# Twelve gated tiles of a fused attention and mixture kernel: split into two f16 words and turned by DMA instead of by TensorE

## The chip, the core and the metric

One Trainium2 chip, of which the kernel uses one core. The metric is the device time of one launch in microseconds (us), taken from the first to the last work of the core. The kernel before was run three times.

## What is computed

The reference is three layers, one after the other; `x` is 2304 tokens (4 batches of 576) by 512.

```python
# layer 0: attention with decay, 4 batches x 8 heads, 576 rows, 64 wide
scores = (q @ k.T) / 8 + cum[:, None] - cum[None, :]      # cum = cumsum(log f); causal mask
x = softmax(scores) @ v                                   # -> [2304, 512]
# layer 1: one dense gated block
h = x @ w_in                                              # w_in [512, 2048]
g = h * sigmoid(1.702 * h)
x = g @ w_out                                             # w_out [2048, 512]
# layer 2: soft mixture of 8 experts, 4 slots each
logits = x @ phi                                          # phi [512, 32]
slots = softmax(logits, over tokens).T @ x                # 32 slots
slot_out[e] = relu(slots[e] @ w1[e]) @ w2[e]
out = softmax(logits, over slots) @ slot_out
```

Layer 1's output is never formed. The kernel folds `w_out @ phi` into one matrix `wphi` [2048, 32], so that the logits of a token are its row of `g` times `wphi`, and it sums the rows of `g` itself for the slots; `w_out` is applied to 32 slot sums at the end.

## The kernel before, in words

The tokens are 18 blocks of 128, and two blocks make a chunk: 9 chunks, 0 to 8. Layer 1 works on a chunk in eight **units** `(t, fg)`: block `t` of the chunk (0 or 1) and a quarter `fg` of the 2048 columns. I number the units through: chunk 2 is units 16 to 23, chunk 4 is 32 to 39, chunk 6 is 48 to 55, the last one is 71. A unit (`moe_steps`, L797) is:

- twelve f16 products `hp` of 128x512 on PE (L814 to L816), three for each of four slices of the inner dimension, since tokens and weights are each held in a high and a low f16 word;
- the gate: `tanh` on ACT (L829), then a product on DVE (L830), which leaves the tile `g`, 128 tokens by 512 in f32;
- later, the **turn** (`turn`, L758): four f32 transposes of 128x128 on PE into one PSUM bank `gT` (L766), and a copy on ACT into `gt` (L773; three buffers);
- later still, the **product with wphi** (`by_phi`, L779): four f32 matmuls whose 32 output columns go to four different groups of 32 PSUM partitions of the tile `p4` (the traces call it `p`, L788). The four groups are added up afterwards (`slot_steps`, L880) by a matmul with `rsum`.

A unit is turned when a later one has been issued, and its product waits for the turn after that (`held`). When all units of a chunk are through, `slot_steps` takes the logits, the softmax over tokens and the slot sums `sp` (L954).

Attention runs interleaved with layer 1: `attend` hands out pieces between the half units, by a table of costs. From the sixth row block on (`late`), a piece (`emit_qk`, L540) is scores on PE, their maximum on DVE (L577), `exp` on ACT (L581), a split of the probabilities into two f16 words `pn` (ACT L589 for the high word, DVE L590 for the low one; two buffers), a DMA transpose into `ph` (L594; three buffers), and the products with `vv` on PE (L632 to L634). The turned queries and keys `kab`, `qa`, `qb` come by DMA transposes too (L347).

All loads and all DMA transposes are issued by SP's queue, in order. The order on each engine is not the order of the code: a scheduler that keeps a timeline of its own sets it when the kernel is built. Each engine then works through its list without overtaking.

The pool `ap_` holds what attention needs, and the buffers `low` of the weight preparation. When the last piece of attention is issued it is closed, and the memory goes to tiles `we` for the expert weights (33 MB in 128 loads, L1109 to L1114), so the first of them waits until attention's tiles are free.

Of the kernel before, what the change touches and what calls it, by code (L numbers as in the profile page):

```python
# [10 lines left out]
F32 = mybir.dt.float32  # L11
# [9 lines left out]
WS = 256.0  # L21
# [9 lines left out]
def attention_moe_softmoe(ctx, tc, q, k, v, f, w_in, w_out, phi, w1, w2, out):  # L31
# [131 lines left out]
    w_at, w_loaded = [0], [0]  # L163
    W_AHEAD = 7

    N_LOW = 2
    RAW_AT = (7, 6, 5, 4, 3, None, None, 7, 6, None, None, 7, None, None, None, None)
    wo_pair = {}

# [28 lines left out]
    def w_first(n):  # L198


        if n in W32:
            nc.scalar.activation(out=W32[n], in_=W32[n], func=AF.Copy, scale=WS)
            return
        words = w_raw.pop(n).rearrange("p (n w) -> p n w", w=2)
        lo, hi = words[:, :, 0], words[:, :, 1]
        val = W32[n] = w32_tile(n)
        low = ap_.tile([128, 512], U32, tag="low", name="low", bufs=N_LOW)
        if n % 2 < 1:
            nc.gpsimd.tensor_scalar(out=val, in0=hi.bitcast(F32), scalar1=2.0 ** -111, scalar2=None, op0=ALU.mult)
        else:  # L210
            nc.scalar.activation(out=val, in_=hi.bitcast(F32), func=AF.Copy, scale=2.0 ** -111)
        nc.scalar.activation(out=low, in_=lo, func=AF.Copy, scale=0.93 * 2.0 ** -29)
        bits = val.bitcast(U32)
        nc.vector.scalar_tensor_tensor(
            out=low, in0=bits, scalar=3, in1=low, op0=ALU.logical_shift_left, op1=ALU.bitwise_or
        )
        nc.vector.scalar_tensor_tensor(
            out=bits, in0=bits, scalar=0x80000000, in1=low, op0=ALU.bitwise_and, op1=ALU.bitwise_or
        )
# [519 lines left out]

    G = {}
    P4 = {}
    held = deque()
# [6 lines left out]
    def units(c):  # L751
# [3 lines left out]
            return [(t, 2 * b + a) for b in range(2) for t in range(2) for a in range(2)]  # L755
        return [(t, fg) for t in range(2) for fg in range(FG)]

    def turn(c, t, fg):  # L758


        g = G[c, t, fg]
        pt = pt2 = ps_mm("gT")
        if (c, t, fg) == (NCH - 1, 1, FG - 1):
            pt2 = ps_sc("gT")
        for a in range(4):
            last_turn[0] = nc.tensor.transpose((pt if a < 2 else pt2)[:, a * 128:(a + 1) * 128], g[:, a * 128:(a + 1) * 128], ident)  # L766
        gt = mp.tile([128, 512], F32, tag="gt", name="gt", bufs=N_GT)
        if (c, t, fg) == (NCH - 1, 1, FG - 1):
            nc.scalar.copy(out=gt[:, halves[0]], in_=pt[:, halves[0]])
            nc.vector.tensor_copy(gt[:, halves[1]], pt2[:, halves[1]])  # L770
            warm(2)
        else:
            nc.scalar.copy(out=gt, in_=pt)  # L773
        with tc.issue_after(last_turn[0].ins):
            while held:
                by_phi(*held.popleft())
        held.append((c, t, fg, gt))
        if c == NCH - 1:
            by_phi(*held.popleft())  # L779

    def by_phi(c, t, fg, gt):
        one = c == NCH - 1
        first = units(c)[0] if not one else (t, 0)
        if (t, fg) == first:
            P4[c, t if one else 0] = (ps_sc if one and t else ps_mi)("p4")
        p4 = P4[c, t if one else 0][:, 0 if one else 128 * t:][:, 0:128]
        for a in range(4):
            last_p4[0] = nc.tensor.matmul(  # L788
                p4[NS * a:NS * (a + 1)], lhsT=wphi[:, 4 * fg + a, :], rhs=gt[:, a * 128:(a + 1) * 128],
                start=((t, fg) == first), stop=(fg == FG - 1), skip_group_check=True,  # L790
            )
        turned[c, t] = turned.get((c, t), 0) + 1
        ts = (t,) if one else (0, 1)
        if all(turned.get((c, i), 0) == FG for i in ts):
            for _ in slot[0]:
                pass
            slot[0] = slot_steps(c, ts)  # L797
            next(slot[0])

    def moe_steps(c):  # L800
        xt = XT[c]
        for u, (t, fg) in enumerate(units(c)):
            if c < 2:
                more_w((max(6, 4 * u + 4) if u < 4 else 16 + 2 * (u - 3)) if c == 0 else 24 + 2 * u + 2)
            hp = ps_mm("hp")
            ts = slice(t * 128, (t + 1) * 128)
            final = (c, u) == (NCH - 1, N_UNIT - 1)
            for kk in range(KD):
                if final and kk == KD - 1:
                    behind = last_turn[0]  # L810
                elif kk % 2 == 0:
                    behind = last_xT.pop(0) if last_xT else None
                with tc.issue_after(behind.ins) if behind else nullcontext():
                    nc.tensor.matmul(hp, lhsT=xt[:, 0, kk, ts], rhs=win(0, fg, kk), start=(kk == 0), stop=False)  # L814
                    nc.tensor.matmul(hp, lhsT=xt[:, 0, kk, ts], rhs=win(1, fg, kk), start=False, stop=False)  # L815
                    last_hp[0] = nc.tensor.matmul(  # L816
                        hp, lhsT=xt[:, 1, kk, ts], rhs=win(0, fg, kk), start=False, stop=(kk == KD - 1)
                    )
                if kk == 1:
                    if final:  # L820
                        while turns:
                            turn(*turns.popleft())
                    yield
            if fg % 2 == 0:
                for half in "ab" if (c, u) == (NCH - 1, 0) else "ab"[fg // 2]:
                    if (c, t, half) not in G:
                        G[c, t, half] = mp.tile([128, 2, 512], F32, tag="g", name="g", bufs=N_G)
            g = G[c, t, fg] = G[c, t, "ab"[fg // 2]][:, fg % 2]
            nc.scalar.activation(out=g, in_=hp, func=AF.Tanh, scale=0.851 / (VS * WS))  # L829
            nc.vector.scalar_tensor_tensor(out=g, in0=g, scalar=1.0, in1=hp, op0=ALU.add, op1=ALU.mult)  # L830
            turns.append((c, t, fg))
            for _ in range(min(3 if c < 2 else 2, len(turns) - 1)):
                if turns[0][2] >= folded[0]:
                    break
                turn(*turns.popleft())
            if c == NCH - 1:
                load_to(RING_AT[u])
            yield
# [4 lines left out]
    def warm(k):  # L843

        if not k:
            return
        if not idle:
            idle.append(ps_pv("z").rearrange("p (k n) -> p k n", k=4))
        for _ in range(k):
            tc.keep_in_program_order(  # L850
                nc.tensor.matmul(
                    idle[0], lhsT=ident16, rhs=ident16.unsqueeze(1).to_broadcast([128, 4, 128]), start=True, stop=True
                )
            )
# [23 lines left out]
    def slot_steps(c, ts=(0, 1)):  # L878
# [3 lines left out]
        end = c == NCH - 1 and ts[-1] == 1  # L882
        l4 = mp.tile([128, 256], F32, tag="l4", name="l4", bufs=1)[:, 0:128 * nt]
        nc.vector.tensor_scalar(
            out=l4, in0=P4.pop((c, ts[0]))[:, 0:128 * nt], scalar1=1.0 / (GS * WS), scalar2=None, op0=ALU.mult
        )
        lg = ps_mi("lg")
        lT = lg[:, 0:128 * nt]
# [477 lines left out]
```

## Time and profile before

| | us |
|---|---|
| median of three runs (lowest, highest) | 548.83 (547.62, 551.03) |
| the profiled execution | 544.7 |
| its span, first to last instruction | 542.2 |

The profiled execution is 4.1 us faster than the median, and what lies around its span is 2.5 us. Busy times are unions of instruction records; matmuls are pipelined, so that records of PE overlap, and what one costs in a full pipe is the distance from its start to the next start, not its length.

### The profile page before, as it was taken

The page shows a single profiled execution, that of the slowest core. Times are in us where ns is not written, and L with a number is a line of the kernel's source. Part 1 is how long each engine was busy: PE and PEld are TensorE (multiplying, and loading weights), DVE is VectorE, ACT ScalarE, POOL GpSimd, SP SyncE. Part 2 cuts the span into 40 slices and gives each one's busy share as a digit, 9 for nine tenths or more (in the row PEclk, how much of TensorE's full clock was granted, in tenths as well). Part 3 has the DMA queues.
Part 4 walks back from the last instruction along what each step waited for, and adds up shares of the span by engine and source line. Part 5 has one row for each costly group of instructions (what it writes and reads, how often), then busy time and mean ns, then how long its engine had stood idle before and what let it go on. Part 6 is the DMA issues. An engine that isn't in the chain of part 4 may idle for free.

```text
span 542.2 us, 13552 instructions
## 1 busy us (share of the span) xinstructions
PE 492.7 (91%) x5353; PEld 309.1 (57%) x5353; DVE 350.4 (65%) x898; ACT 310.6 (57%) x607; POOL 71.5 (13%) x123
## 2 busy tenths in 40 slices
PE   3467899999889999999999999989999999999982
PEld 3456776866567555655665657556665555454531
DVE  8988979778666447667677868877675413360132
ACT  5867686778667446556666667576664323221211
POOL 4866754311000000010000001000000000000000
PEclk9969799999999999999999999999999999999997
DMA  9998763999959307997739699994554499989998
GB/s 242 285 376 149 200 129 133 272 191 204 169 105 168 61 19 139 185 181 139 125 77 181 116 189 176 212 156 88 93 105 90 132 383 367 348 308 367 337 327 269
DMA packets 230847, 105.62 MB, mean 195 GB/s; under 512 B 202593, under 2 KB 213345, under 8 KB 230785
## 3 DMA queue, kind: packets, MB, share of 16 engines
q1 hardware_dynamic: 229552, 103.59, 80.3%
q10 hardware_dynamic: 1232, 1.18, 0.7%
q8 instruction: 42, 0.69, 0.6%
q14 instruction: 21, 0.16, 0.1%
HBM read 64.63 MB, written 4.72 MB: 128 GB/s over the span
## 4 chain that ended last, share of the span: by engine, by line
PE 65%; DMA 15%; DVE 9%; ACT 4%; SPq 2%; issue 2%; POOL 0%; DVEq 0%; ACTq 0%; POOLq 0%
PE hp L814 10%; PE hp L815 9%; PE hp L816 9%; DMA ph<-pn 6%; PE gT L766 5%; PE p L788 4%; DMA we<-in_moe_w_dram 3%; PE pv L626 3%; PE l L1227 3%; PE sp L954 3%; PE pv L632 2%; DMA kf<-in_k_dram 2%; PE scs L554 2%; DMA kab<-kan 2%; PE scs L555 2%
## 5 line engine op out<-in xcount | busy, mean ns | idle before, releaser
L814 PE MATMUL hp<-w,xt 128*128 128x512 f16 x288 | 109.6, 381 | 0.6 <-DVE g L830 0.6
L815 PE MATMUL hp<-w,xt 128*128 128x512 f16 x288 | 109.2, 379 | 0.0
L816 PE MATMUL hp<-w,xt 128*128 128x512 f16 x288 | 109.2, 379 | 0.0
L581 ACT ACTIVATE pf<-scs,mx 128x512 f32<-128x512 f32 (+3 forms) x108 | 57.3, 541 | 38.7 <-DVE mx L577 29.4
L830 DVE SCALAR_TENSOR_TENSOR g<-g,hp 128x512 f32<-128x512 f32 x72 | 49.2, 683 | 43.9 <-ACT g L829 43.7
L590 DVE SCALAR_TENSOR_TENSOR pn<-pf,pn 128x512 f16<-128x512 f32 (+2 forms) x78 | 51.2, 658 | 32.1 <-ACT pn L589 31.4
L829 ACT ACTIVATE g<-hp 128x512 f32<-128x512 f32 x72 | 42.5, 590 | 47.4 <-PE hp L816 47.3
L589 ACT ACTIVATE pn<-pf 128x512 f16<-128x512 f32 (+2 forms) x78 | 47.3, 607 | 22.3 <-DMA ph<-pn 19.8
L577 DVE CUSTOM_DVE_ANT_0 scs<-scs,zmq 128x128 f32<-128x128 f32 (+3 forms) x96 | 46.6, 496 | 6.8 <-PE scs L555 4.2
L773 ACT COPY gt<-gT 128x512 f32<-128x512 f32 x71 | 41.1, 582 | 10.7 <-PE gT L766 10.5
L816 PEld LDWEIGHTS <-xt 128*128 128x128 f16 x288 | 28.2, 98 | 32.9
L632 PE MATMUL pv<-vv,ph 128*128 128x65 f16 (+1 forms) x360 | 41.8, 196 | 5.3 <-DMA ph<-pn 4.2
L814 PEld LDWEIGHTS <-xt 128*128 128x128 f16 x288 | 28.8, 100 | 28.8 <-issue 5.0
L766 PE MATMUL gT<-ident,g 128*128 128x128 f32 x288 | 45.0, 277 | 0.0
L766 PEld LDWEIGHTS gT<-ident,g 128*128 128x128 f32 x288 | 34.0, 141 | 14.8 <-issue 3.5
L632 PEld LDWEIGHTS <-ph 128*128 128x128 f16 (+1 forms) x360 | 33.8, 102 | 14.6 <-issue 7.0
L815 PEld LDWEIGHTS <-xt 128*128 128x128 f16 x288 | 28.2, 98 | 23.7 <-issue 1.1
L633 PE MATMUL pv<-vv,ph 128*128 128x65 f16 (+1 forms) x360 | 41.7, 195 | 0.0
L634 PE MATMUL pv<-vv,ph 128*128 128x65 f16 (+1 forms) x360 | 41.4, 194 | 0.0
L588 POOL MEMSET pn<- 128x128 f16 x12 | 2.5, 205 | 252.6 <-DMA ph<-pn 250.8
L633 PEld LDWEIGHTS <-ph 128*128 128x128 f16 (+1 forms) x360 | 34.1, 102 | 2.5 <-issue 0.6
L554 PE MATMUL scs<-kab,qa 128*128 128x128 f16 x240 | 34.4, 220 | 0.5 <-ACT pf L581 0.5
(233 smaller groups left out, 1017.3 us busy)
## 6 DMA issues: line engine op xcount, KB each, us to landing
we<-in_moe_w_dram SPq DMA_DIRECT2D x127, 256.0 KB, 5.5
raw<-in_moe_w_in_dram SPq DMA_DIRECT2D x16, 512.0 KB, 7.2
raw<-in_moe_w_out_dram SPq DMA_DIRECT2D x16, 512.0 KB, 5.7
kf<-in_k_dram SPq DMA_DIRECT2D x13, 256.0 KB, 3.3
qf<-in_q_dram SPq DMA_DIRECT2D x13, 256.0 KB, 3.7
vf<-in_v_dram SPq DMA_DIRECT2D x12, 256.0 KB, 4.2
out_dram<-ob SPq DMA_DIRECT2D x12, 256.0 KB, 3.5
ph<-pn SPq DMA_TRANSPOSE x78, 3.0
```

Source lines behind the costliest of these rows:

```text
L554: nc.tensor.matmul(o, lhsT=QA[r][:, h, :], rhs=KA[base + j][:, h, :], start=True, stop=False)
L577: nc.vector.tensor_tensor_reduce(out=o, in0=o, in1=mask, scale=-SC, scalar=3.0e38 if n == 128 else DG[r][1][:, u], op0=ALU.add, op1=ALU.mi ...
L581: nc.scalar.activation(out=pf[:, hh * nb:(hh + 1) * nb], in_=o, func=AF.Exp, bias=mx[:, hh:hh + 1], scale=-1.0)
L589: nc.scalar.activation(out=pn[:, 0, 0:w], in_=pf, func=AF.Copy, scale=PB)
L590: nc.vector.scalar_tensor_tensor(out=pn[:, 1, 0:w], in0=pf, scalar=PB, in1=pn[:, 0, 0:w], op0=ALU.mult, op1=ALU.subtract)
L632: nc.tensor.matmul(o, lhsT=ph[0:rr, 0, off:off + n], rhs=vh, start=(j == 0), stop=False)
L633: nc.tensor.matmul(o, lhsT=ph[0:rr, 0, off:off + n], rhs=vl, start=False, stop=False)
L766: last_turn[0] = nc.tensor.transpose((pt if a < 2 else pt2)[:, a * 128:(a + 1) * 128], g[:, a * 128:(a + 1) * 128], ident)
L814: nc.tensor.matmul(hp, lhsT=xt[:, 0, kk, ts], rhs=win(0, fg, kk), start=(kk == 0), stop=False)
L815: nc.tensor.matmul(hp, lhsT=xt[:, 0, kk, ts], rhs=win(1, fg, kk), start=False, stop=False)
L816: last_hp[0] = nc.tensor.matmul(hp, lhsT=xt[:, 1, kk, ts], rhs=win(0, fg, kk), start=False, stop=(kk == KD - 1))
L830: nc.vector.scalar_tensor_tensor(out=g, in0=g, scalar=1.0, in1=hp, op0=ALU.add, op1=ALU.mult)
```

## The change

In twelve units, three each of chunks 2 and 4 (units 17, 19, 21 and 33, 35, 37) and six of chunk 6 (49 to 54), `stage` follows the gate at once: ACT writes the high f16 word of `g` times 2^-8 into `gh`, DVE the low word, and SP issues one DMA transpose of 128x1024 f16 into a buffer of `gt`. In `turn` these units have no transposes on PE and no copy on ACT; their product (`by_phi_halves`) is eight f16 matmuls: four with 64 output columns (both words of `wphi` with the high word of `g`) and four with 32 (the high word of `wphi` with the low word of `g`). They add into the same `p4`, over its four groups of partitions. `split_wphi` makes the two words of `wphi` once. The other units of these chunks scale by 2^-8 in their copy, and the scale is taken out of the logits. `gh` and the words of `wphi` lie in the two `low` buffers, which the weight preparation has left by then.

```diff
+    BY_DMA = {2: (1, 3, 5), 4: (1, 3, 5), 6: (1, 2, 3, 4, 5, 6)}
+    TS = 2.0 ** -8
...
+    def split_wphi():
+        wphl.append(ap_.tile([128, 512], F32, tag="low1", name="wphl").bitcast(F16).rearrange(
+            "p (k h s) -> p k h s", k=KF, h=2))
+        nc.scalar.activation(out=wphl[0][:, :, 0], in_=wphi, func=AF.Copy)
+        nc.vector.tensor_tensor(out=wphl[0][:, :, 1], in0=wphi, in1=wphl[0][:, :, 0], op=ALU.subtract)
+
+    def stage(c, t, fg):
+        g = G[c, t, fg]
+        gh = ap_.tile([128, 512], F32, tag="low0", name="gh").bitcast(F16).rearrange("p (h n) -> p h n", h=2)
+        nc.scalar.activation(out=gh[:, 0], in_=g, func=AF.Copy, scale=TS)
+        nc.vector.scalar_tensor_tensor(
+            out=gh[:, 1], in0=g, scalar=TS, in1=gh[:, 0], op0=ALU.mult, op1=ALU.subtract
+        )
+        gt = mp.tile([128, 512], F32, tag="gt", name="gt", bufs=N_GT).bitcast(F16)
+        nc.sync.dma_start_transpose(
+            out=gt.rearrange("p (a q) -> p a q", q=128), in_=gh.rearrange("p h n -> p (h n)")
+        )
+        staged[c, t, fg] = gt
+
+    def by_phi_halves(p4, fg, gt, stop):
+        gt = gt.rearrange("p (h a q) -> p h a q", h=2, a=4)
+        for both, a, g0 in ((1, 0, 0), (1, 1, 2), (0, 0, 0), (0, 1, 1), (0, 2, 2), (0, 3, 3), (1, 2, 0), (1, 3, 2)):
+            w = wphl[0][:, 4 * fg + a, 0:1 + both].rearrange("p h s -> p (h s)")
+            last_p4[0] = nc.tensor.matmul(
+                p4[NS * g0:NS * (g0 + 1 + both)], lhsT=w, rhs=gt[:, 1 - both, a],
+                start=False, stop=stop, skip_group_check=True,
+            )
...
+        if (c, t, fg) in staged:
+            with tc.issue_after(last_hp[0].ins):
+                while held:
+                    by_phi(*held.popleft())
+            held.append((c, t, fg, staged.pop((c, t, fg))))
+            return
...
+            if u in BY_DMA.get(c, ()):
+                if not wphl:
+                    split_wphi()
+                stage(c, t, fg)
```

**PE, the end of unit 54 in chunk 6 (`hp` is the unit's last product).** Before, the turn and the product of earlier units follow, and then attention's scores:

```order
L816 MATMUL hp<-w,xt 128x512
L766 MATMUL gT<-ident,g 128x128 x4
L788 MATMUL p_6012<-gt,wphi 32x128 x4
L565 LDWEIGHTS qa
L565 MATMUL scs<-kab,qa 64x128
```

Now there is no turn, and the eight f16 products stand between two units' `hp`, with their own weight loads:

```order
L857 MATMUL hp<-w,xt 128x512
L784 LDWEIGHTS wphl
L784 MATMUL p_6030<-gt,wphl 64x128
L784 LDWEIGHTS wphl
L784 MATMUL p_6030<-gt,wphl 64x128
L784 LDWEIGHTS wphl
L784 MATMUL p_6030<-gt,wphl 32x128
...
L784 MATMUL p_6030<-gt,wphl 64x128
L855 LDWEIGHTS xt
L855 MATMUL hp<-w,xt 128x512
```

The turn is gone from PE's list; the output columns of its neighbours go from 128 to 64 to 32 to 64 and back to 128.

**SP, from the last row block's keys to the first expert weights (chunk 6).** Before:

```order
L594 DMA_TRANSPOSE ph<-pn 128x6x128 x6
L347 DMA_TRANSPOSE qa<-qan 128x8x64
L347 DMA_TRANSPOSE qb<-qbn 128x8x64
L594 DMA_TRANSPOSE ph<-pn 128x6x128
L594 DMA_TRANSPOSE ph<-pn 128x8x128 x8
L594 DMA_TRANSPOSE ph<-pn 128x10x128 x4
L1109 DMA we<-in_moe_w_dram 128x512 x64
```

Now:

```order
L775 DMA_TRANSPOSE gt<-gh 128x8x128
L593 DMA_TRANSPOSE ph<-pn 128x8x128 x2
L775 DMA_TRANSPOSE gt<-gh 128x8x128
L593 DMA_TRANSPOSE ph<-pn 128x8x128 x2
L775 DMA_TRANSPOSE gt<-gh 128x8x128
L593 DMA_TRANSPOSE ph<-pn 128x8x128 x2
L775 DMA_TRANSPOSE gt<-gh 128x8x128
L593 DMA_TRANSPOSE ph<-pn 128x8x128
L593 DMA_TRANSPOSE ph<-pn 128x10x128 x4
L1155 DMA we<-in_moe_w_dram 128x512 x64
```

After every second `ph` a `gt` has been put into the same queue, and the expert weights still come last.

**ACT, units 51 and 52 of chunk 6.** Before, the copy of a turned tile stands behind each `tanh`; now a split does, which must wait for DVE's half of the gate and for the one buffer `gh`:

```order
L870 ACTIVATE g<-hp 128x512
L588 ACTIVATE pn<-pf 128x384
L588 ACTIVATE pn<-pf 128x512
L580 ACTIVATE pf<-scs,mx 128x512
L770 ACTIVATE gh<-g 128x512
L580 ACTIVATE pf<-scs,mx 128x512
L870 ACTIVATE g<-hp 128x512
L588 ACTIVATE pn<-pf 128x512 x2
L580 ACTIVATE pf<-scs,mx 128x512
L770 ACTIVATE gh<-g 128x512
```

What stands behind `gh<-g` in this list is attention's `exp` and `pn`, and the next unit's `tanh`.

## Rows read from the trace of the kernel before

**Rows 1.** The page's first part: busy us, share, instructions.
```profile
PE 492.7 (91%) x5353; PEld 309.1 (57%) x5353; DVE 350.4 (65%) x898; ACT 310.6 (57%) x607; POOL 71.5 (13%) x123
```

**Rows 2.** Two stretches: length, busy us, clock, DMA share, GB/s.
```profile
170.00:430.00 260.00, 255.55 (x2889) 154.41 (x2886) 177.08 (x486) 159.07 (x322) 5.56 (x32) 1.00 0.70 128
430.00:542.00 112.00, 97.63 (x931) 47.66 (x929) 33.35 (x94) 27.58 (x58) 0.53 (x1) 0.97 0.98 337
```

**Rows 3.** PE's longest wait from 170 to 430 us: us, times, longest.
```profile
PE pv L632 <- DMA ph<-pn: 2.2, 3, 0.9
```

**Rows 4.** Timeline of PE in chunk 4: start, length, instruction.
```profile
285.54 0.60 PE L766 MATMUL gT<-ident,g 128*128 128x128 f32 x4
285.98 0.22 PE L554 MATMUL scs<-kab,qa 128*128 128x128 f16 x1
...
286.86 0.19 PE L633 MATMUL pv<-vv,ph 128*128 128x65 f16 x1
286.89 0.19 PE L634 MATMUL pv<-vv,ph 128*128 128x65 f16 x1
287.01 0.42 PE L788 MATMUL p<-gt,wphi 128*32 128x128 f32 x8
287.37 0.20 PE L632 MATMUL pv<-vv,ph 128*128 128x65 f16 x1
...
291.81 1.92 PE L954 MATMUL sp<-g,dd 128*32 128x512 f32 x16
293.67 0.66 PE L766 MATMUL gT<-ident,g 128*128 128x128 f32 x4
```

**Rows 5.** The same view in chunk 6, where scores have 64 output columns.
```profile
398.43 0.60 PE L766 MATMUL gT<-ident,g 128*128 128x128 f32 x4
398.96 0.43 PE L788 MATMUL p<-gt,wphi 128*32 128x128 f32 x8
399.31 0.25 PE L565 MATMUL scs<-kab,qa 128*64 128x128 f16 x2
399.39 0.22 PE L569 MATMUL scs<-kab,qb 128*64 128x128 f16 x2
399.45 0.22 PE L565 MATMUL scs<-kab,qa 128*64 128x128 f16 x2
```

**Rows 6.** Groups by line: busy us, mean ns of one, idle before, releasers.
```profile
L773 ACT COPY gt<-gT 128x512 f32<-128x512 f32 x71 | 41.1, 582 | 10.7 <-PE gT L766 10.5
L590 DVE SCALAR_TENSOR_TENSOR pn<-pf,pn 128x512 f16<-128x512 f32 x42 | 28.9, 688 | 14.7 <-ACT pn L589 14.5
L589 ACT ACTIVATE pn<-pf 128x512 f16<-128x512 f32 x42 | 26.4, 631 | 13.0 <-DMA ph<-pn 12.1
```

**Rows 7.** Stretches of 20 us in chunk 2 and chunk 6; columns as in rows 2.
```profile
180.00:200.00 20.00, 20.00 (x180) 10.72 (x173) 8.36 (x19) 8.78 (x18) 0.00 (x0) 1.00 0.18 41
...
380.00:400.00 20.00, 20.00 (x267) 12.44 (x263) 15.14 (x37) 12.75 (x23) 0.00 (x0) 1.00 0.64 104
400.00:420.00 20.00, 20.00 (x244) 12.10 (x243) 10.90 (x25) 11.04 (x22) 0.83 (x4) 1.00 0.44 86
```

**Rows 8.** Timeline of SP's queue: start, time of all, instruction and count.
```profile
381.13 38.19 SPq L594 DMA_TRANSPOSE ph<-pn  x13
426.42 44.27 SPq L1109 DMA_DIRECT2D we<-in_moe_w_dram  x64
```

**Rows 9.** Tile `ph`, 361 to 420 us: issue ns, PE's wait, ACT's, landing.
```profile
L594 SPq DMA_TRANSPOSE ph<-pn x20: 1210/1235/2055, 360.5 to 418.0; - x20
...
  DMA ph<-pn: 1.9, 2
...
  ACT pn L589: 7.6, 8
...
DMA to landing us min/median/max: 2.5/2.9/4.2
```

**Rows 10.** ACT's timeline: `tanh` of units 50 and 52.
```profile
369.95 0.58 ACT L829 ACTIVATE g<-hp 128x512 f32<-128x512 f32 x1
...
381.37 0.59 ACT L829 ACTIVATE g<-hp 128x512 f32<-128x512 f32 x1
```

More of the change, by code (lines that the diff above doesn't have):

```diff
@@ L164, in attention_moe_softmoe @@
     W_AHEAD = 7
-    N_LOW = 2
     RAW_AT = (7, 6, 5, 4, 3, None, None, 7, 6, None, None, 7, None, None, None, None)
@@ L206, in w_first @@
         val = W32[n] = w32_tile(n)
-        low = ap_.tile([128, 512], U32, tag="low", name="low", bufs=N_LOW)
+        low = ap_.tile([128, 512], U32, tag=f"low{n % 2}", name="low")
         if n % 2 < 1:
@@ L737, in attn_items @@
         return [(cost, fn, args) for _, _, cost, fn, args in items]
+    BY_DMA = {2: (1, 3, 5), 4: (1, 3, 5), 6: (1, 2, 3, 4, 5, 6)}
+    TS = 2.0 ** -8
+    wphl = []
+    staged = {}
     G = {}
@@ L771, in turn @@
             warm(2)
+        elif c in BY_DMA:
+            nc.scalar.activation(out=gt, in_=pt, func=AF.Copy, scale=TS)
         else:
@@ L786, in by_phi @@
         p4 = P4[c, t if one else 0][:, 0 if one else 128 * t:][:, 0:128]
-        for a in range(4):
+        if gt.dtype == F16:
+            by_phi_halves(p4, fg, gt, fg == FG - 1)
+        for a in range(4) if gt.dtype == F32 else ():
             last_p4[0] = nc.tensor.matmul(
@@ L884, in slot_steps @@
         nc.vector.tensor_scalar(
-            out=l4, in0=P4.pop((c, ts[0]))[:, 0:128 * nt], scalar1=1.0 / (GS * WS), scalar2=None, op0=ALU.mult
+            out=l4, in0=P4.pop((c, ts[0]))[:, 0:128 * nt], scalar1=1.0 / (GS * WS * (TS if c in BY_DMA else 1.0)),
+            scalar2=None, op0=ALU.mult
         )
```

## The prediction

> **What bounds the kernel now.** I began with busy shares. PE leads with 91% [rows 1]; DVE and ACT are busy 65% and 57%. A share over the whole span says little, so I cut the span where the expert weights begin. From 170 to 430 us, which holds chunks 2 to 6 and so all twelve units, PE is busy 255.55 of 260.00 us at a granted clock of 1.00, the upper level of 2.4 GHz; the DMA engines are at 0.70 [rows 2]. From 430 us on the DMA engines are at 0.98 and PE at 97.63 of 112 [rows 2]: there the expert weights set the pace. So this is a kernel of two bounds in a row. The hinge is in SP's queue: the first load of expert weights is issued at 426.42 us, behind the last `ph` of attention [rows 8], and 64 loads in 44.27 us leave no gap after it. What PE saves before attention ends therefore brings the whole train of loads forward, one for one, if attention itself ends earlier.
>
> Does it? In PE's list the last product of attention stands behind 714 of the 864 `hp` matmuls, before and after the change alike (counted in the order). All twelve staged products stand ahead of it, the last of them just after unit 56, so the words of `wphi`, which share memory with the expert tiles, don't hold the loads up either.
>
> The third view is waits: in the stretch PE's longest one, for `ph`, is 2.2 us in 3 times [rows 3]. PE is nearly gapless; but attention's own loop is tight, see below.
>
> **What PE loses and gains.** Starts, not lengths, give the price. Four transposes run from 285.54 to 285.98, 0.44 us; where the f32 product follows they take 0.53 (398.43 to 398.96) [rows 4, 5]. The 0.09 between the two is the step from 128 to 32 output columns: the same step from `pv` to `p` is 0.12 where two `pv` are 0.03 apart (286.86, 286.89, 287.01) [rows 4]. So I take 0.44 for the transposes alone: 12 x 0.44 = **5.3 us** removed.
>
> The f32 product takes 0.36 us, 287.01 to 287.37 [rows 4]. The slot sums are eight matmuls of the same kind with 512 columns instead of 128, in 1.86 us (291.81 to 293.67) [rows 4], so four of 128 stream in 1.86 / 8 = 0.23, and 0.13 is the step back to 128. The new product is eight f16 matmuls of 128 columns. Two f16 matmuls of 64 output columns in different halves take 0.06 together (399.39 to 399.45) [rows 5]. If the four of 32 share the array in the same way, the eight take three times 0.06 = 0.18; if nothing overlaps, 8 x 0.06 = 0.48. I take 0.18, because the pairs are the nearest row: 12 x (0.23 - 0.18) = **0.6 us** saved; the other end is 3.0 us lost.
>
> Then the steps between 128, 64 and 32 output columns. The new product goes 64, 32, 64, and the scheduler has cut four of the twelve in two, with attention's work between the parts. I counted the steps in PE's list over units 15 to 59: 170 before, 182 now. It is only 12 more, since the old product of each staged unit had steps as well. At 0.09 to 0.13 each, say 0.1, this is **1.2 us** lost. The Trainium skill has a rule that speaks against this change here (TensorEngine Tiling (Array Packing), Key Properties): changing the tiling mode, not just the tile, drains the TensorE. The rows agree for 128 to 32; no row shows 64 to 32 by itself. By the rule the sum holds as it stands; without it, it would be 1.2 us better.
>
> PE's sum: 5.3 + 0.6 - 1.2 = **4.7 us** saved. The ends: 12 x 0.53 + 0.6 = 7.0 if the steps cost nothing; and 5.3 - 3.0 - 24 x 0.1 = -0.1, nothing, if the eight don't overlap and each has two steps of its own.
>
> **ACT and DVE.** ACT loses twelve copies of 582 ns and gets twelve splits, nearest row 631 ns [rows 6]: 0.6 us more in 159. DVE gets twelve low words of 688 ns [rows 6], 8.3 us on 177 of 260 [rows 2]. Making the words of `wphi` costs one such pair, once. As load, all this is covered by PE. What counts is the place: behind each split in ACT's list stand `exp`, `pn` and the next `tanh`, and the split waits for DVE's gate and for the one buffer `gh`. From the end of a unit's `hp` to the landing of its transpose I sum 0.58 (`tanh`) + 0.69 + 0.63 + 0.69 + 2.9 = 5.5 us [rows 6, 9, 10], the gate on DVE put at the low word's price. Two units take 11.4 us in chunk 6 (369.95 to 381.37) [rows 10], and PE's list has each staged product about two units after its `hp`. That leaves about 6 us for SP's queue. The next split comes 5.7 us after the last; it is ready to write 0.58 + 0.69 = 1.3 us into its unit, 7.0 us on this count, when `gh` has been read at 5.5. So it fits, by 1.5 us, in chunk 6; in chunks 2 and 4 every second unit is staged, and it fits easily.
>
> **SP and DMA.** Twelve transposes more. An issue holds SP for 1235 ns, and a transpose lands 2.9 us after its issue [rows 9]. From 380 to 420 us the DMA engines are busy (0.64 + 0.44) x 20 = 21.6 us [rows 7], with 13 `ph` and one `qb` issued: at most 1.5 us each. Six more in chunk 6 are 9 us there, which takes a share of 0.54 to about 0.77; chunk 2 begins at 0.18 [rows 7]. Capacity is there. Latency is the dearer thing: SP's queue doesn't overtake, and in chunk 6 a `gt` stands behind every second `ph`. ACT already waits 7.6 us in 8 times for `ph` to free a buffer of `pn`, between 361 and 420 us, and of that 1.9 us reaches PE [rows 9]: a quarter. If each of the six `gt` makes one `ph` later by an issue, 6 x 1.235 = 7.4 us more for ACT, a quarter of it is **1.9 us** of PE's time. Below, it is nothing, if each `gt` falls into a gap of SP (13 issues of 1.235 us fill 16 of the 38.19 us [rows 8, 9]); above, all twelve by a whole transpose, 12 x 1.5 = 18 us. I take 1.9, the row's own proportion. Chunks 2 and 4 I charge nothing, as almost all of PE's wait for `ph` (1.9 of 2.2 us) [rows 3, 9] lies in chunk 6.
>
> **Sum.** 4.7 - 1.9 = 2.8 us less: the profiled execution would go from 544.7 to 541.9. The median of the runs is 548.83, so I say **546.0**.
>
> **Rivals.**
>
> *PE's saving in full.* The steps of columns cost little, the eight overlap, each `gt` finds a gap in SP: 7.0 us, and something on top, because `gT` no longer takes one of three PSUM banks that it shares with `hp`. For it: SP is issuing for less than half of the time in chunk 6. Against: ACT's waits there. 548.8 - 7.0 = 541.8, and down to 540.
>
> *The queue becomes the bound, and it gets slower.* In chunk 6 attention runs in a loop: `pn` has two buffers, ACT fills one, DVE completes it, SP issues, it lands, and only then may ACT go on. Each `gt` in SP's queue that waits for its own low word on DVE holds the `ph` behind it, the held `pn` stops ACT, behind which stands the next `tanh`, and PE runs dry. Each `gt` then costs a whole 1.5 us, or more where it waits. It decides when more than about seven of twelve hit: 7 x 1.5 = 10.5 us, against 4.7 saved, is 5.8 us slower. With nine it is 13.5 - 4.7 = 8.8 us: 557.6. For it: the loop's wait of 7.6 us, and PE's list, which can't go around a late `pv`. Against: PE has had only 2.2 us of such waits in 260, and only six units are staged in the tight place.
>
> *It does not do what it says.* The eight matmuls take as long as the four transposes and the f32 product they replace (PE's lower end, -0.1), or the loads of expert weights don't come earlier. Then 549, with the loss of 1.9 us at most 551.
>
> **How the numbers follow.** A measurement of this kernel tells 1%, 5.5 us, from no change. The forecast's own case, 542.5 to 548, has 0.52, of which 0.04 is below 543.3. PE's saving in full has 0.28, all faster by over 1%. No effect has 0.07, within 1%. The slower case has 0.13. Faster is 0.04 + 0.28 = 0.32; within 1% is 0.48 + 0.07 = 0.55; slower is 0.13. A range that leaves out the slower case and a little of the fastest is 540 to 552; it takes in PE's upper end (541.8) and the case of no effect with its loss (551).
>
> **What would show it.** Right: in PE's timeline no `gT` between the staged units, the eight f16 matmuls spanning about 0.2 to 0.4 us from the first start to the next work; expert loads beginning some 3 us before 426.4; the span from there to the end unchanged. The charge: ACT's wait for `ph` between 361 and 420 us grown from 7.6 to about 15, PE's from 1.9 to about 4. Wrong towards faster: PE's waits not grown, and loads from 420 us or earlier. Wrong towards slower: PE waiting for `gt` or `ph` by 10 us in chunk 6, ACT standing before `gh`, SP before a `gt` that DVE has not finished.

## The result and the profile after

| us | before | after |
|---|---|---|
| median of 20 runs each (lowest, highest) | 549.44 (547.09, 552.89) | 552.74 (549.04, 555.52) |
| the profiled execution | 544.7 | 554.3 |
| its span | 542.2 | 551.9 |

The ratio is 1.0053 [1.0036, 1.0071]: the change makes the kernel slower by 0.5%, 3.3 us on the medians. That is within 1%, but of the other sign than the forecast, and 0.7 us above the range. The two profiles lie 9.7 us of span apart, three times as much; the experiments show why.

Busy us of the engines, from the page of after, beside [rows 1]:

```profile
PE 495.7 (90%) x5305; PEld 307.9 (56%) x5305; DVE 356.1 (65%) x911; ACT 311.9 (57%) x608; POOL 72.0 (13%) x123
```

PE has 48 instructions fewer and is yet busy for 3.0 us more. The same two stretches as in [rows 2], cut at 430 us, in the same columns:

```profile
170.00:430.00 260.00, 248.95 (x2795) 148.81 (x2795) 181.47 (x491) 162.72 (x325) 5.52 (x32) 1.00 0.80 141
430.00:552.00 122.00, 108.84 (x1058) 54.28 (x1054) 37.80 (x109) 31.08 (x66) 0.53 (x1) 0.98 0.93 316
```

From 170 to 430 us PE stands idle for 11.05 us, against 4.45 before. The expert loads say how far behind attention ends (SP's timeline; start, time of all, instruction, count):

```profile
415.64 1.25 SPq L775 DMA_TRANSPOSE gt<-gh  x1
417.60 11.87 SPq L593 DMA_TRANSPOSE ph<-pn  x5
437.38 44.27 SPq L1155 DMA_DIRECT2D we<-in_moe_w_dram  x64
```

The first load comes at 437.38 instead of 426.42 us [rows 8]. From there to the end of the span it is 114.5 us, and was 115.8: that part is as forecast, and the loss lies ahead of it. But where? I took the start of each unit's `tanh` from the traces. Unit 12 starts at 168.49 us before and at 177.19 after, and at unit 16 after is 8.0 us behind. The first staged unit is 17. In this pair of profiles most of the loss stands ahead of all that the prediction priced.

### The profile page after: what moved, and what is told of

Read it like the earlier page. It is cut to its first block, busy times and chain, and to the rows that moved or that the text cites. A ratio compares the mean times of both kernels' runs of the same rounds, so it can differ in the third digit from the quotient of the medians.

```text
span 551.9 us, 13499 instructions
## 1 busy us (share of the span) xinstructions
PE 495.7 (90%) x5305; PEld 307.9 (56%) x5305; DVE 356.1 (65%) x911; ACT 311.9 (57%) x608; POOL 72.0 (13%) x123
## 4 chain that ended last, share of the span: by engine, by line
PE 58%; DMA 17%; DVE 11%; ACT 6%; issue 3%; SPq 2%; POOL 0%; DVEq 0%; ACTq 0%; POOLq 0%
PE hp L855 9%; PE hp L856 8%; PE hp L857 8%; DMA ph<-pn 7%; PE gT L803 3%; DMA kab<-kan 3%; PE l L1273 3%; PE sp L1000 3%; PE p L829 2%; DMA kf<-in_k_dram 2%; DMA we<-in_moe_w_dram 2%; DMA raw<-in_moe_w_out_dram 2%; PE pv L631 2%; PE pv L625 2%; DVE low L213 2%
## 5 line engine op out<-in xcount | busy, mean ns | idle before, releaser
L855 PE MATMUL hp<-w,xt 128*128 128x512 f16 x288 | 111.2, 386 | 0.3 <-DVE g L871 0.3
L856 PE MATMUL hp<-w,xt 128*128 128x512 f16 x288 | 110.8, 385 | 0.0
L857 PE MATMUL hp<-w,xt 128*128 128x512 f16 x288 | 110.5, 384 | 0.0
L631 PE MATMUL pv<-vv,ph 128*128 128x65 f16 (+1 forms) x360 | 42.5, 197 | 8.6 <-DMA ph<-pn 7.9
L631 PEld LDWEIGHTS <-ph 128*128 128x128 f16 (+1 forms) x360 | 34.0, 102 | 18.5 <-DMA ph<-pn 11.0
L632 PE MATMUL pv<-vv,ph 128*128 128x65 f16 (+1 forms) x360 | 42.2, 196 | 0.0
L633 PE MATMUL pv<-vv,ph 128*128 128x65 f16 (+1 forms) x360 | 41.9, 195 | 0.0
L803 PE MATMUL gT<-ident,g 128*128 128x128 f32 x240 | 36.8, 277 | 0.3 <-DVE g L871 0.3
L554 PE MATMUL scs<-kab,qb 128*128 128x128 f16 x240 | 34.5, 220 | 1.6 <-DMA qb<-qbn 1.6
L632 PEld LDWEIGHTS <-ph 128*128 128x128 f16 (+1 forms) x360 | 34.3, 103 | 2.3 <-issue 0.4
L633 PEld LDWEIGHTS <-ph 128*128 128x128 f16 (+1 forms) x360 | 34.4, 103 | 1.6 <-issue 1.2
```

Source lines behind the costliest of these rows:

```text
L631: nc.tensor.matmul(o, lhsT=ph[0:rr, 0, off:off + n], rhs=vh, start=(j == 0), stop=False)
L632: nc.tensor.matmul(o, lhsT=ph[0:rr, 0, off:off + n], rhs=vl, start=False, stop=False)
L633: nc.tensor.matmul(o, lhsT=ph[0:rr, 1, off:off + n], rhs=vh, start=False, stop=(j == i))
L857: last_hp[0] = nc.tensor.matmul(hp, lhsT=xt[:, 1, kk, ts], rhs=win(0, fg, kk), start=False, stop=(kk == KD - 1))
```

## The experiments

Theories at the start. **A, the list:** the weight preparation's two buffers `low` had one tag with two buffers and now have two tags with one each. That line, which the prediction never speaks of, gives the scheduler another order from unit 6 on, and this is the loss. **B, the staging:** the twelve splits, transposes and products cost more than the turns they replace. The order by itself already shows that the two can be parted: the line of the tags alone gives the order of after up to the middle of unit 19; staging with the old tag (the words of `wphi` and one `gh` taken from it) keeps that of before up to unit 19.

In the table, durations are from the `tanh` of the first unit named to that of the second, in one profile each. The last column is unit 71's `tanh`, from the span's start.

| kernel | order ahead of unit 17 | 5 to 12 | 16 to 24 | 24 to 47 | 47 to 71 | unit 71 |
|---|---|---|---|---|---|---|
| before | old | 73.3 | 42.7 | 129.3 | 113.8 | 475.5 |
| f1_before_again | old | 74.8 | 43.0 | 132.7 | 113.9 | 483.6 |
| g1_before_third | old | 72.7 | 43.1 | 129.2 | 113.8 | 475.9 |
| e1_tags | new | 77.6 | 44.2 | 130.4 | 113.6 | 483.4 |
| after | new | 79.9 | 41.6 | 132.1 | 115.0 | 486.4 |
| f3_tags_stage_6 | new | 78.6 | 44.4 | 129.8 | 110.9 | 483.3 |
| e2_stage | old | 73.1 | 39.9 | 135.1 | 114.0 | 478.5 |
| e3_stage_2_4 | old | 72.4 | 39.9 | 135.0 | 120.0 | 485.3 |
| e4_stage_6 | old | 74.2 | 43.9 | 133.4 | 111.3 | 480.1 |
| f2_stage_6_w64 | old | 73.3 | 43.0 | 130.3 | 111.2 | 474.2 |
| f4_stage_6_no_dma | old | 73.8 | 43.4 | 130.5 | 113.2 | 478.0 |
| g2_stage_w64 | old | 74.2 | 39.6 | 133.8 | 118.1 | 484.2 |

Some of these durations hold stretches in which PE's granted clock was at its lower level, 1.2 GHz, and that differs between profiles of one kernel: before shows 1.00 from 64 to 535 us, f1_before_again 0.83 from 144 to 154 and again from 324 to 334 us. What the clock took is, as an estimate that takes PE to be the limit throughout, (1 - granted clock) x length: 1.7 us for 10 us at 0.83. By it, 5 to 12 holds 1.7 us in f1_before_again, e4_stage_6 and f4_stage_6_no_dma, 3.4 in e1_tags and f3_tags_stage_6, and 5.1 in after. From 24 to 47 it is 1.7 us in f1_before_again and 3.4 in e4_stage_6. From 47 to 71 it is 1.7 us in e2_stage, e3_stage_2_4 and f2_stage_6_w64, and 3.4 in g2_stage_w64. The other entries hold none. These are the stretches from 47 to 71 in e2_stage, in f2_stage_6_w64 and in g2_stage_w64 (two), columns as in [rows 2]:

```profile
365.00:375.00 10.00, 8.37 (x87) 5.20 (x87) 7.58 (x19) 7.38 (x16) 0.00 (x0) 0.83 0.67 131
```

```profile
360.00:370.00 10.00, 8.09 (x69) 5.12 (x67) 6.88 (x20) 7.01 (x14) 0.00 (x0) 0.83 0.88 140
```

```profile
365.00:375.00 10.00, 8.12 (x71) 4.85 (x70) 7.49 (x19) 7.14 (x14) 0.00 (x0) 0.83 0.70 142
385.00:395.00 10.00, 7.13 (x79) 4.55 (x77) 7.26 (x22) 6.38 (x13) 0.00 (x0) 0.83 0.64 132
```

**e1_tags: before with the line of the tags alone.** No unit is staged.

```diff
-        low = ap_.tile([128, 512], U32, tag="low", name="low", bufs=N_LOW)
+        low = ap_.tile([128, 512], U32, tag=f"low{n % 2}", name="low")
```

> The kernel before with one line changed: the two buffers of the weight preparation are two tags of one buffer each instead of one tag of two. Nothing is staged. The scheduler's lists then are those of the changed kernel up to the middle of unit 19, and differ from the kernel before from unit 6 on. Theory A (the loss lies in the order of units 6 to 19, which the tags alone bring): about 6 us slower than before, 553 to 557, with unit 12's tanh some 8 us later than before's 168.5 us, and a stretch of the lower clock between 135 and 160 us. Theory B (the loss lies in the staged units, their transposes in SP's queue): within 1.5 us of before.

Measured: 552.04 us against 549.18, ratio 1.0066 [1.0033, 1.0099]. This line alone costs what the whole change costs. It is 2.9 us on the medians, and unit 12's `tanh` comes 6.1 us later than in the first profile of before: less than theory A said, and outside theory B. On PE the list of e1_tags joins that of before again in unit 23. What the line moves on SP, from about 119 us on (- of before, + with two tags):

```order
 L347 DMA_TRANSPOSE kab<-kbn 128x8x128
 L347 DMA_TRANSPOSE qa<-qan 128x8x128
-L594 DMA_TRANSPOSE ph<-pn 128x8x128
 L347 DMA_TRANSPOSE qb<-qbn 128x8x128
 L307 DMA kf<-in_k_dram 128x8x64
-L307 DMA vf<-in_v_dram 128x8x64
 L307 DMA qf<-in_q_dram 128x8x64
 L594 DMA_TRANSPOSE ph<-pn 128x8x128 x2
+L307 DMA vf<-in_v_dram 128x8x64
 L347 DMA_TRANSPOSE kab<-kan 128x8x128
 L347 DMA_TRANSPOSE kab<-kbn 128x8x128
+L594 DMA_TRANSPOSE ph<-pn 128x8x128 x2
```

The first transposed probabilities stand behind `qb` and two loads of the next row block. SP's timeline, first of before, then of e1_tags:

```profile
122.92 1.27 SPq L594 DMA_TRANSPOSE ph<-pn  x1
...
127.93 3.08 SPq L594 DMA_TRANSPOSE ph<-pn  x2
```

```profile
125.96 2.72 SPq L594 DMA_TRANSPOSE ph<-pn  x2
...
132.80 3.94 SPq L594 DMA_TRANSPOSE ph<-pn  x2
```

The queues of the two run within 0.2 us of each other until then, and the first `ph` goes out 3 us later. PE's wait for `ph` from 118 to 160 us, in before and in e1_tags (us, times, longest):

```profile
PE pv L632 <- DMA ph<-pn: 1.9, 2, 1.4
```

```profile
PE pv L632 <- DMA ph<-pn: 3.9, 2, 2.2
```

And three stretches around it, columns as in [rows 2], in before and in e1_tags:

```profile
130.00:140.00 10.00, 9.00 (x119) 6.35 (x117) 7.35 (x23) 8.01 (x17) 0.00 (x0) 1.00 1.18 192
140.00:150.00 10.00, 8.46 (x102) 5.32 (x100) 6.92 (x19) 7.00 (x16) 0.00 (x0) 1.00 0.90 148
150.00:160.00 10.00, 8.78 (x136) 6.65 (x132) 7.46 (x28) 7.36 (x17) 0.00 (x0) 1.00 0.52 110
```

```profile
130.00:140.00 10.00, 7.38 (x115) 5.29 (x109) 7.44 (x24) 6.77 (x16) 0.00 (x0) 0.96 1.09 170
140.00:150.00 10.00, 8.31 (x83) 5.26 (x82) 6.72 (x21) 6.69 (x14) 0.00 (x0) 0.84 0.91 161
150.00:160.00 10.00, 10.00 (x116) 6.22 (x116) 5.24 (x14) 5.62 (x11) 0.00 (x0) 0.85 0.36 81
```

First PE is busy for 1.6 us less, then the granted clock falls from 1.00 to 0.84. PE is busy for nearly the same time (26.24 and 25.69 us of 30) and does 314 matmuls instead of 357, with 24 `hp` among them instead of 31. PE's timeline of e1_tags shows the clock change in one row of `hp` products of one size:

```profile
140.13 0.63 PE L816 MATMUL hp<-w,xt 128*128 128x512 f16 x1
140.56 0.63 PE L814 MATMUL hp<-w,xt 128*128 128x512 f16 x1
...
142.92 0.38 PE L814 MATMUL hp<-w,xt 128*128 128x512 f16 x1
143.13 0.38 PE L815 MATMUL hp<-w,xt 128*128 128x512 f16 x1
```

The starts are 0.43 us apart, then 0.21: the lower level, 1.2 GHz, and the upper one, 2.4 GHz. So in this profile the late `ph` is followed by waiting and then by slow products. All three profiles of the new order take 77.6 to 79.9 us for units 5 to 12, all nine of the old one 72.4 to 74.8. A lower clock is not peculiar to the new order: e4_stage_6, f4_stage_6_no_dma and f1_before_again show 0.83 to 0.84 from 140 to 150 us as well, and with 73.8 to 74.8 us they are still 3 us below the new one. In these three PE's one wait for `ph` from 133 to 150 us was 1.6 to 1.8 us long, in the other six profiles of the old order, whose clock stayed at 1.00, 1.1 to 1.4. The new order adds waits, and in all three of its profiles the clock is below 0.90 in at least one of these stretches. What decides whether a wait is followed by the lower clock isn't shown: f3_tags_stage_6 waits for 2.1 us near 140 us and keeps 1.00 until 150.

How much is waiting, and how much clock? With the clock's estimate taken off, units 5 to 12 take 74.2 to 75.2 us in the new order and 72.1 to 74.2 in the old one, 1.8 us more on the means; the clock's own part is 3.4 us more. Over all timed runs, and not the profiles alone, the mean granted clock was 0.972 in e1_tags and 0.974 in before beside it, which by the same estimate is about 1 us; in f3_tags_stage_6 it was 0.969 against 0.975, about 3 us. So the lower clock is a part of the price, and how large a part is not settled.

**e2_stage: twelve units staged, old tag.** The rest is the changed kernel's.

```diff
-        low = ap_.tile([128, 512], U32, tag=f"low{n % 2}", name="low")
+        low = ap_.tile([128, 512], U32, tag="low", name="low", bufs=2)
...
-        gh = ap_.tile([128, 512], F32, tag="low0", name="gh").bitcast(F16).rearrange("p (h n) -> p h n", h=2)
+        if len(wphl) < 2:
+            wphl.append(ap_.tile([128, 512], F32, tag="low", name="gh", bufs=2).bitcast(F16).rearrange(
+                "p (h n) -> p h n", h=2))
+        gh = wphl[1]
```

> All twelve units staged as in the change, but the weight preparation keeps its one tag of two buffers, and the words of wphi and gh take these two once it is through. The lists are those of the kernel before up to unit 19. Theory A: the twelve units by themselves are a gain, PE's 0.44 us less for each turn and 0.16 more for each product (0.52 against 0.36 in the changed kernel's trace), 12 x 0.28 = 3.4 us, of which the queue takes up to 3 back: 546 to 549. Theory B: 3 us slower than before, 552 to 554, like the changed kernel.

Measured: 547.96 against 549.18, ratio 0.9979 [0.9948, 1.0009]; units 5 to 12 are back at 73.1 us, and the time is inside theory A's 546 to 549. The product of the two ratios, 1.0066 x 0.9979 = 1.0045, lies in after's interval. So the tags are the loss, and staging by itself is worth between -2.9 and +0.5 us: the prediction's -2.8 is just inside, but the gain isn't shown.

**e3_stage_2_4 and e4_stage_6: e2_stage with a part of the units.**

```diff
-    BY_DMA = {2: (1, 3, 5), 4: (1, 3, 5), 6: (1, 2, 3, 4, 5, 6)}
+    BY_DMA = {2: (1, 3, 5), 4: (1, 3, 5)}
```

> As the kernel with the twelve units staged under the old order of the weight preparation, but with the six units of chunks 2 and 4 alone. Theory A: 6 x 0.28 = 1.7 us faster than before, 0 to 3. Theory B, in its form that every staged unit costs: 1.5 us slower; in the form that only the dense chunk 6 costs: the same as before.

```diff
-    BY_DMA = {2: (1, 3, 5), 4: (1, 3, 5), 6: (1, 2, 3, 4, 5, 6)}
+    BY_DMA = {6: (1, 2, 3, 4, 5, 6)}
```

> As the kernel with the twelve units staged under the old order, but with the six units of chunk 6 alone; PE's list is that of the kernel before up to unit 51. Theory A: between 1.7 us faster and 2 us slower than before, the queue taking what PE saves. Theory B: 3 us slower than before, all of the change's loss.

Measured: chunks 2 and 4 alone 553.72, ratio 1.0109 [1.0066, 1.0152]; chunk 6 alone 547.06, 0.996 [0.9932, 0.9989]. The first, 4.5 us slower, is a miss for both theories; the second, 2.1 us faster, goes a little beyond theory A. The tight place gains and the roomy ones lose. In the table, the four kernels that stage chunks 2 and 4 take 39.6 to 41.6 us for units 16 to 24, the other eight 42.7 to 44.4: 3.2 us less on the means (40.3 and 43.5). From 24 to 47 they take 3.3 us more (134.0 and 130.7; with the clock's estimate off 3.9 more, and the groups, 132.1 to 135.1 and 129.2 to 131.0, don't overlap). The lists show what moved: by the end of unit 23 e2_stage, e3_stage_2_4 and after have 360 products `pv` behind them, before and e4_stage_6 420, and by unit 47 all five have 888. Part of attention has moved out of the first stretch into the second, and no time is won. e3_stage_2_4 then loses once more in chunk 6 (120.0 us from 47 to 71, of which the clock took 1.7), where nothing is staged and its list has 1020 `pv` done by unit 53 instead of 984. PE's wait from 320 to 420 us, and two stretches, in e3_stage_2_4:

```profile
PE pv L631 <- DMA ph<-pn: 4.7, 5, 1.9
```

```profile
380.00:390.00 10.00, 8.38 (x102) 5.57 (x99) 6.47 (x23) 5.84 (x14) 0.00 (x0) 0.99 0.64 107
390.00:400.00 10.00, 10.00 (x105) 5.30 (x103) 6.71 (x16) 5.79 (x11) 0.00 (x0) 0.84 0.59 94
```

It is the pattern of e1_tags again: waits for `ph`, then the lower clock.

**f1_before_again, g1_before_third: the kernel before, profiled again.**

> The kernel before, unchanged, profiled once more on the chip of this set. Theory A holds that the profiled execution of 544.7 us was one of the fastest of its kind (the median of 29 runs is 549.2), and that a typical one reaches unit 45 some 4 us later than the 347.75 us seen there, by waits for ph or by stretches of the lower clock at places that vary. Theory B: it agrees with the first profile within 1.5 us at every unit.

> The kernel before, unchanged, profiled a third time. Two profiles of it differ by 8 us at unit 47, most of it between units 0 and 5 and between 24 and 45, where nothing differs in the lists. If that is the kernel's own spread, the third lies between or near them before unit 47, and from unit 47 to unit 71 it takes the same time as both, within 0.5 us.

Measured: spans of 549.1 and 541.6 us, beside 542.2. One kernel gives profiles 7.5 us apart. f1_before_again reaches unit 45 8.4 us later than the first profile, twice what its theory A said, and g1_before_third 0.8 us later, so the first profile does not stand alone. From 47 to 71 the three agree within 0.1 us, as was expected. The difference lies up to unit 12 and from 24 to 47, and most of it is the clock: 0.969 over 549.1 us in f1_before_again and 0.978 over 542.2 in the first, which by the estimate is 5.1 of the 6.9 us between them. So the 9.7 us between the profiles of before and after were the 3.3 us of the medians and a profile of before that was among its fastest; the lower clock in units 5 to 12 of after is, by the estimate, 5.1 of them. Here are the waits of f1_before_again from 170 to 440 us, beside [rows 3]:

```profile
PE pv L632 <- DMA ph<-pn: 3.6, 3, 1.8
PE lg L893 <- DVE l L884: 1.1, 1, 1.1
```

Its wait for `ph` is 3.6 us and not 2.2: a difference of 1 or 2 us in such a row tells nothing on two profiles.

**f3_tags_stage_6: the changed kernel with chunk 6 staged alone, two tags.**

```diff
-    BY_DMA = {2: (1, 3, 5), 4: (1, 3, 5), 6: (1, 2, 3, 4, 5, 6)}
+    BY_DMA = {6: (1, 2, 3, 4, 5, 6)}
```

> The changed kernel with the six units of chunk 6 alone, under the two tags. Theory A: the tags' 2.9 us and the gain of chunk 6, 2.1 us, add up: 549 to 551, and the three units each of chunks 2 and 4 are what takes the changed kernel from there to 552.7. Against it: if chunk 6 gains only under the old order, 552 or more.

Measured: 548.23 against 547.07, ratio 1.0007 [0.9976, 1.0038], 0.6% below the 1.0066 of the tags alone, where e4_stage_6 gains 0.4% in the old order. The median is 1.2 us above that of before beside it, where theory A's sum has 2.9 - 2.1 = 0.8. The product of the two ratios, 1.0066 x 0.996 = 1.0026, lies in the interval, so the two effects may simply add up; and on top of the tags, too, chunks 2 and 4 bring no gain (1.0053 with them).

**f4_stage_6_no_dma: e4_stage_6 without its six transposes.** The splits write into `gt` themselves, and the product reads them as they are: the turn of six tiles is left out. SP's list is then that of before.

```diff
-        gh = wphl[1]
+        gt = mp.tile([128, 512], F32, tag="gt", name="gt", bufs=N_GT).bitcast(F16)
+        gh = gt.rearrange("p (h n) -> p h n", h=2)
...
-        nc.sync.dma_start_transpose(
-            out=gt.rearrange("p (a q) -> p a q", q=128), in_=gh.rearrange("p h n -> p (h n)")
-        )
```

> The six units of chunk 6 staged under the old order, but ACT and DVE write the two words straight into gt, and the six DMA transposes are left out (the product then takes untransposed words, so the output is not the reference's). SP's list is that of the kernel before. If the six transposes in SP's queue cost about 2 us, as the prediction charged, 1.5 to 2.5 us faster than the six units staged with them, 545; if they fall into gaps of the queue, the same within 1 us, 547.

Measured: 546.32 against 547.07, ratio 0.9978 [0.9947, 1.0009]; with the transposes it was 0.996. Units 47 to 71 take 113.2 us without them and 111.3 with them. Taking the transposes out of SP's queue gains nothing that shows. A charge of 1.9 us, 0.35%, can't be excluded by these intervals, but nothing points to it. The comparison is not of the transposes alone: PE's lists of the two kernels differ between units 53 and 58, and that is where f4_stage_6_no_dma falls behind. From unit 47 to 55 it takes 41.0 us and e4_stage_6 41.4, to unit 58 58.4 and 56.3.

**f2_stage_6_w64: e4_stage_6 with all eight matmuls 64 columns wide.** Both words of `wphi` meet both words of `g`, so that no step from 64 to 32 columns is left inside the product.

```diff
-        for both, a, g0 in ((1, 0, 0), (1, 1, 2), (0, 0, 0), (0, 1, 1), (0, 2, 2), (0, 3, 3), (1, 2, 0), (1, 3, 2)):
-            w = wphl[0][:, 4 * fg + a, 0:1 + both].rearrange("p h s -> p (h s)")
+        for h, a in ((0, 0), (0, 1), (0, 2), (0, 3), (1, 0), (1, 1), (1, 2), (1, 3)):
+            g0 = 2 * (a % 2)
+            w = wphl[0][:, 4 * fg + a].rearrange("p h s -> p (h s)")
```

> The six units of chunk 6 staged under the old order, and the product as eight f16 matmuls that all have 64 output columns (both words of wphi with the low word of g as well), so that no step between 64 and 32 columns lies inside it. If those steps cost 0.1 us each, the product spans 0.35 to 0.4 us instead of the 0.52 seen in the changed kernel, 6 x 0.15 = 0.9 us less than with 64, 32, 64: 545.5 to 547. If they cost nothing, it spans 0.5 us and the time stays at that of the six units staged, 547.

Measured: 543.92 against 547.07, ratio 0.9928 [0.9899, 0.9958]. This is the fastest kernel here, 0.7% faster than the one before; beside e4_stage_6 (0.996) the intervals overlap, and PE's lists of the two differ between units 54 and 59, so that the product's 6 x 0.17 = 1.0 us need not be all of it. PE's timeline, first of after, then of f2_stage_6_w64:

```profile
419.84 0.60 PE L803 MATMUL gT<-ident,g 128*128 128x128 f32 x4
420.37 0.59 PE L784 MATMUL p<-gt,wphl 128*64 128x128 f16 x8
420.89 0.39 PE L855 MATMUL hp<-w,xt 128*128 128x512 f16 x1
```

```profile
388.40 0.41 PE L788 MATMUL p<-gt,wphl 128*64 128x128 f16 x8
388.75 0.39 PE L859 MATMUL hp<-w,xt 128*128 128x512 f16 x1
```

From start to start the product takes 0.52 us in after and 0.35 with 64 columns throughout: the two steps inside cost 0.17 us together, and the product spans what was expected. (The ratio is a little beyond what was expected, 545.5 to 547 of the 549.18 that it was reckoned from, 0.9933 to 0.996.) The single records of after's trace show where: four matmuls of 32 columns start within 0.01 us of each other, and before the first and after the last of them 0.17 and 0.16 us pass between two starts, where 0.05 to 0.08 us pass from one pair of 64 to the next in f2_stage_6_w64.

**g2_stage_w64: the same product in e2_stage, all twelve units.**

> All twelve units staged under the old order, the product with 64 output columns throughout. If the three units each of chunks 2 and 4 are worth what PE saves on them, 6 x 0.43 = 2.6 us, it beats the six units of chunk 6 alone in this form (0.9928 of before): 0.988. If they are worth nothing, or bring an order that costs as much, 0.993 to 0.998.

Measured: 549.82 against 547.18, ratio 1.0039 [1.0009, 1.0069]: a miss. Twelve units with the shorter product come out slower than with the longer one in e2_stage; the two intervals just meet. Its list is another one again, from unit 20 on, and PE's wait for `ph` from 170 to 440 us is the longest of all:

```profile
PE pv L631 <- DMA ph<-pn: 8.4, 10, 2.3
PE p L833 <- ACT dT L966: 1.8, 1, 1.8
```

Chunk 6's gain, 2.5 to 2.9 us from 47 to 71 in the three kernels that stage it alone with its transposes, doesn't show in the same way with twelve units (114.0, 115.0, 118.1). A part of that is the clock: with its estimate off they take 112.2, 115.0 and 114.6 us against 113.8 before, so that e2_stage keeps a gain of 1.6 and the other two have none. Over all its timed runs g2_stage_w64 has a mean granted clock of 0.970 against 0.974, by the estimate about 2 of the 2.6 us that it is slower.

## Why the prediction was wrong

**The step that failed** is the comparison of the orders. The prediction says that in PE's list the last product of attention stands behind 714 of 864 `hp`, "before and after the change alike", and goes on from there to price pieces. One place that agrees doesn't make the lists agree: they part in unit 6, well ahead of the first staged unit, 17, by a line that staged nothing. That term is 0.0066 x 549.2 = +3.6 us by e1_tags (1.8 to 5.4 by its interval), and what the profiles of the new order have in common is the late `ph` in SP's queue, PE's longer waits for it and more of the lower clock behind them; how the loss divides between the two is open. The prediction had no term for it, and none of its rivals did; its rival on the slower side put the loss into SP's queue in chunk 6.

**PE's saving** was put at 4.7 us. The new product takes 0.52 us up to the next work, where the prediction had 0.41: 0.18 for the matmuls, 0.13 for the step back and one step of 0.1 more per unit; 0.44 + 0.36 - 0.52 = 0.28 us is saved per unit, 12 x 0.28 = 3.4. The mechanism was right, the four matmuls of 32 columns do share the array, and a size was off: the two inner steps cost more than the one step of 0.1 that was counted. The Trainium skill (TensorEngine Tiling (Array Packing), Key Properties) says that a change of the tiling mode drains the TensorE, and the trace agrees: the two inner steps cost 0.17 us together. Above all, the saving shows in the time only where chunk 6 alone was staged. That ACT's and DVE's additional load is covered by PE stands: they were busy for 1.3 and 5.7 us more by the page.

**The queue's charge** of 1.9 us was to show as ACT's wait for `ph` going from 7.6 to about 15 us in chunk 6, and PE's from 1.9 to about 4. Tile `ph` of after, 361 to 431 us, who waited for it (us, times):

```profile
  ACT pn L588: 8.8, 7
...
  PE pv L631: 1.5, 3
```

Neither grew as foretold, and f4_stage_6_no_dma found no gain in leaving the transposes out, though with another order on PE. The fit of the staged chain was nearer the edge than its 1.5 us of slack: ACT waited 3.1 us for `gh` in 2 times. Tile `gh` of after, its issues, ACT's wait and the landing:

```profile
L775 SPq DMA_TRANSPOSE gt<-gh x12: 1231/1256/2009, 204.3 to 415.6; - x12
...
  ACT gh L770: 3.1, 2
...
DMA to landing us min/median/max: 2.7/2.8/4.9
```

**"Chunks 2 and 4 I charge nothing"** was wrong as well, for a reason that no row of before could give: staging there changes what the scheduler puts where. 3.2 us won in units 16 to 24 are lost again as 3.3 us from 24 to 47, and staging in twelve units is not better than in six (after 1.0053, f3_tags_stage_6 1.0007; e2_stage 0.9979, e4_stage_6 0.996; the pairs' intervals meet or overlap, all signs agree, and g2_stage_w64 beside f2_stage_6_w64, 1.0039 to 0.9928, are clear of each other).

**Right** were the two bounds in a row, with the hinge at the first expert load, and the span from there to the end (115.8 before, 114.5 after, 113.5 in e2_stage; 114.6 and 114.8 in the two other profiles of before).

**Open** is why two tags with one buffer each make the scheduler choose another order than one tag with two: that they do is shown, the cause lies in its own timeline, which no run looks into. Nor is it settled why chunk 6's gain shrinks or goes when chunks 2 and 4 are staged too: the lists differ, PE's waits for `ph` are longer (5.0 us in e2_stage, 8.4 in g2_stage_w64, from 170 to 440 us), and in both profiles the granted clock falls to 0.83 over 10 us near 370 us. Nor is it shown by itself how much of the tags' loss is the lower clock.

## What to carry to other kernels

Where a scheduler sets the order, compare the whole lists, above all ahead of the first edited instruction, and build the edit's side lines (a tag, a buffer count) as kernels of their own: one such line cost 0.66% here, more than staging all twelve units was worth (0.2%, not clear of nothing). Profile the kernel before more than once before reading a stage, as two of its own profiles lay 7.5 us apart, and look at the granted clock in each stage before comparing its length. And stage in parts: six units in the old order, with one width of output columns, gained 0.7%, where all twelve in the same form lost 0.4%.

## What the runs showed of the hardware

A DMA transpose of 128x1024 f16 landed 2.8 us (median) after its issue and held SP for 1.26 us, and leaving six of them out of a busy stage gained nothing that a timing of 0.3% could see. In e1_tags PE's clock fell to its lower level behind a stretch in which it was busy for 7.38 of 10 us and waited for `ph` by at most 2.2 us at a time, and `hp` then ran 0.43 instead of 0.21 us apart. By the estimate of the table the clock took 1.6 us from 140 to 150 us and 1.5 from 150 to 160 (granted clock 0.84 and 0.85), beside 3.9 us of waiting for `ph`. Eight f16 matmuls, four of 64 and four of 32 output columns, took 0.52 us, and eight of 64 took 0.35: the wider ones, which compute more, were faster.
